# The u products of the first batch move behind its first gating product, in a fused linear attention and gated MLP kernel

## The chip, the cores and the metric

One core of a Trainium2 chip runs the whole kernel. The metric is the device time of one execution, in microseconds, as the median of several executions. PE, ACT, DVE, POOL and SP are the engines of the core: TensorE, ScalarE, VectorE, GpSimd and SyncE. Each works through its own queue of instructions in the order in which the program issued them, and waits on semaphores for the others.

## The reference

For 4 batches of 768 positions, 8 heads of 48 features. All data are f32.

```
f = 1 / (1 + exp(-f_logit))
for t in range(768):                       # per batch and head
    state = f[t][:, None] * state + outer(k[t], v[t])
    y[t] = q[t] @ state
x = y, heads joined                        # (4, 768, 384)
h = gelu(x @ w_in)                         # w_in: 384 x 1024
u, v = h[..., :512], h[..., 512:]
v_n = (v - mean(v)) / sqrt(var(v) + 1e-6) * g_ln
v_s = w_sg @ v_n + b_sg                    # over positions, w_sg: 768 x 768
out = x + (u * v_s) @ w_out                # w_out: 512 x 384
```

## The kernel before

The work is cut into 24 tiles of 128 positions (n, six to a batch) and 8 groups of three tiles (g, two to a batch). For each tile the attention is done in chunked form: the gates (exp, log, a triangular product `cum`, two exp), k and q scaled by them on DVE or POOL, transposes on PE (`tr`), scores and state updates (`su`, lines 474 and 479), mask on DVE (line 484), and the output (`y`, line 522), which ACT and DVE join into x (lines 526 and 530). x is transposed (`xT`, line 552) and split into a high part in fp32r (`xh`, ACT) and a low part (`xl`, DVE, line 569).

Every large product is done as three products in fp32r, high by high, high by low and low by high, in `mm3` (line 547). For each tile `hv` is x against the second half of `w_in` (nine products of 512 columns), and after it come gelu, statistics, normalisation (`nh`, lines 598 and 599 on DVE) and the low part (`nl`, line 604). For each group `hu0..3` are x against the first half of `w_in` (nine products of 384 columns each), and `sg0..3` are the gating products over all six tiles of the batch against `w_sg` (18 products each). `po` is the output product of a tile. A gating product needs the normalised v of all six tiles of its batch, but no u; u is needed by what follows a gating product (`sm_`, line 636, on POOL or DVE).

The weights must be prepared on the chip in the first batch. `w_in` comes in 8 chunks (0 to 3 are for u, 4 to 7 for v) and `w_out` in 4. Each chunk goes through `wa` (ACT, line 300), `wb` (DVE, lines 306 to 308), `wc` (DVE, lines 312 and 313), `wd` (line 318, POOL or DVE), `we` (ACT) and `wf` (line 334, POOL or DVE). `w_sg` is transposed on PE in 12 halves (`wT`, line 343) and split by ACT (line 782) and DVE (line 783).

The order of all instructions is written by a planner, `Plan`, that runs when the program is built. Every step has a cost on each engine that may do it, what it needs, rings of buffers that it takes and frees, and a due time. The planner goes through time and gives an engine the step with the least due time among those that could start about now. Its costs are numbers in the code. In the first batch due times are `T_FIRST + T_TILE * n` and offsets from it: `hv` comes 9 after its tile's transposes, the `hu` of a group 2 after its last `hv`, the `wT` with the second group's `hu`, and the gating products after all of these. The later batches' attention is merged into the products of the batch before by `merge(units + rest, att, A0, A1)`.

Of the kernel before, what the change touches and what calls it, by code (L numbers as in the profile page):

```python
# [36 lines left out]
A0, A1 = 0.12, 0.66  # L37
T_FIRST, T_TILE = 8.0, 6.0
# [14 lines left out]
class Plan:  # L53
# [46 lines left out]
    def run(self):  # L100
        self.dues()
        free = dict.fromkeys(("PE", "ACT", "DVE", "POOL", "SP"), 0.0)
        small, table, wire = False, "E", 0.0
# [102 lines left out]
    STAY, HOLD, SHIFT = 2.0, 4.0, 0.8  # L206
# [3 lines left out]
def gla_moe_kernel(ctx: ExitStack, tc: tile.TileContext, q, k, v, f, w_in, g_ln, w_sg, b_sg, w_out, cst, out):  # L210
# [109 lines left out]
    def w_dst(key):  # L320
        kind, c = key
        a = w_tmp[key][1].bitcast(F32)
        if kind == "in":
            sl = slice(c * P, (c + 1) * P)
            return w_in_hi[:, :, sl], w_in_lo[:, :, sl], a.rearrange("p (k c) -> p k c", k=KT)
# [228 lines left out]
    def x_slice(n):  # L554
        if n // GR not in xT:
# [65 lines left out]
    def sgu(g, ft):  # L621
# [4 lines left out]
            [((v_hl[n0 + s][0][:, fs], v_hl[n0 + s][1][:, fs]), (w_sg_hi[:, s, tokens(g)], w_sg_lo[:, s, tokens(g)])) for s in range(NT)],  # L626
# [68 lines left out]
    def pe(name, fn, t, needs, small=False, bank=1, **kw):  # L695
        add(name, lambda e: fn(), {"PE": t}, 0.2, needs, small=small, bank=bank, **kw)
# [88 lines left out]

    for n in range(N):
# [204 lines left out]
```

## Time and profile before

| what | value |
|---|---|
| runs shown | 393.88, 393.95 and 395.94 us, median 393.95 us |
| the profiled execution | 393.7 us, of which the span is 391.8 us |
| PE busy | 370.2 us, 94% |
| DVE, ACT, POOL busy | 244.6, 170.5, 170.9 us |
| mean granted clock of TensorE | 0.984 |

Busy time is the time in which an engine had an instruction in work. The end of a matrix product is modelled, so a busy PE is not a PE at its best rate. A share of the whole span hides that the stages differ: the first hundred microseconds, with the attention of the first batch and the weights, are unlike the rest.

### The profile page before, as it was taken

The numbers are of one execution on the slowest core, as the hardware profiler recorded it, in microseconds if no ns is written. First come the engines' busy times: TensorE is split into PE (matmuls) and PEld (weight loads), VectorE is DVE, ScalarE is ACT, GpSimd is POOL, SyncE is SP. The second block draws the span as 40 slices with busy tenths as digits, with TensorE's granted clock in tenths as the row PEclk, the third lists the DMA queues.
The fourth block names the chain that finished last, engine by engine and source line by source line (L and its number), as shares of the span: only waits on it lengthen the run. The fifth ranks groups of instructions, "written<-read, shape, count | busy, mean of one in ns | idle before, by whom it ended". The sixth has DMA issues, their size and how long they took to land.

```text
span 391.8 us, 11353 instructions
## 1 busy us (share of the span) xinstructions
PE 370.2 (94%) x4774; PEld 342.0 (87%) x4774; DVE 244.6 (62%) x464; ACT 170.5 (44%) x360; POOL 170.9 (44%) x208
## 2 busy tenths in 40 slices
PE   4879989889899999999999999999999999999994
PEld 3757878779799998999998989899999989899994
DVE  1699995894897566462765576454757665553331
ACT  5376737446653542327553443237544433311110
POOL 2264564423754445162644445052736534233220
PEclk9977999999999999999999999999999999999998
DMA  9999864540137796100187765000376000000002
GB/s 190 219 222 227 166 178 94 123 152 0 23 63 146 127 154 117 33 0 22 22 146 142 115 118 100 20 22 0 56 142 119 10 22 2 21 22 0 22 21 86
DMA packets 133324, 33.90 MB, mean 87 GB/s; under 512 B 125588, under 2 KB 131860, under 8 KB 133268
## 3 DMA queue, kind: packets, MB, share of 16 engines
q1 hardware_dynamic: 133268, 33.12, 41.6%
q8 instruction: 39, 0.64, 0.7%
q14 instruction: 17, 0.14, 0.1%
HBM read 28.34 MB, written 4.77 MB: 84 GB/s over the span
## 4 chain that ended last, share of the span: by engine, by line
PE 76%; DVE 14%; ACT 3%; DMA 2%; issue 2%; POOL 1%; SPq 1%; POOLq 0%
PE ps_b L547 56%; PE ps_y L522 5%; PE ps_b L455 5%; PE ps_s L474 3%; DVE wt L313 2%; PE ps_b L552 2%; PE ps_s L479 2%; DVE wt L312 2%; DMA dec<-dec_d 1%; DVE wt L308 1%; ACT f_raw L234 1%; DVE w_sg_lo L783 1%; DMA f_raw<-in_f_logit_dram 1%; PE ps_b L440 1%; DVE vh L598 1%
## 5 line engine op out<-in xcount | busy, mean ns | idle before, releaser
L547 PE MATMUL ps_b<-w_sg_hi,vh 128*128 128x384 f32 x192 | 65.8, 342 | 1.0 <-DVE gt L631 1.0
L547 PE MATMUL ps_b<-w_sg_hi,vl 128*128 128x384 f32 x192 | 64.6, 336 | 0.0
L547 PE MATMUL ps_b<-w_sg_lo,vh 128*128 128x384 f32 x192 | 64.6, 336 | 0.0
L636 POOL TENSOR_TENSOR gt<-gt,u 128x384 f32<-128x384 f32 x31 | 32.0, 1033 | 65.4 <-DVE gt L631 41.8
L547 PE MATMUL ps_b<-w_out_hi,gg 128*128 128x384 f32 x174 | 48.8, 341 | 0.0
L604 POOL TENSOR_TENSOR vl<-vg,vh 128x512 fp32r<-128x512 f32 x24 | 31.0, 1292 | 18.1 <-DVE vg L599 18.1
L547 PEld LDWEIGHTS ps_b<-w_sg_hi,vh 128*128 128x128 f32 x192 | 36.1, 188 | 2.0 <-DVE gt L631 1.8
L631 DVE SCALAR_TENSOR_TENSOR gt<-ps_b,cols,b_bc 128x384 f32<-128x384 f32 x32 | 19.7, 614 | 26.8 <-PE ps_b L547 25.6
L547 PEld LDWEIGHTS ps_b<-w_sg_lo,vh 128*128 128x128 f32 x192 | 36.1, 188 | 0.0
L547 PEld LDWEIGHTS ps_b<-w_sg_hi,vl 128*128 128x128 f32 x192 | 36.1, 188 | 0.0
L239 ACT COPY sk<-ps_b 112x512 f32<-112x512 f32 x41 | 22.5, 589 | 28.3 <-PE ps_b L455 28.1
L547 PE MATMUL ps_b<-xTh,w_in_hi 128*128 128x384 f32 x96 | 33.1, 345 | 1.4 <-ACT u L234 1.4
L522 PE MATMUL ps_y<-vs,st 64*64 64x48 f32 x768 | 31.4, 223 | 1.2 <-DVE st L484 1.2
L547 PE MATMUL ps_b<-w_in_hi,xTh 128*128 128x512 f32 x72 | 31.2, 433 | 1.3 <-DVE xTl L569 1.3
L547 PE MATMUL ps_b<-xTh,w_in_lo 128*128 128x384 f32 x96 | 32.3, 336 | 0.0
L547 PE MATMUL ps_b<-xTl,w_in_hi 128*128 128x384 f32 x96 | 32.1, 335 | 0.0
L522 PEld LDWEIGHTS ps_y<-vs,st 64*64 64x64 f32 x768 | 28.7, 138 | 3.9 <-DVE st L484 1.4
L547 PEld LDWEIGHTS ps_b<-w_out_hi,gg 128*128 128x128 f32 x174 | 31.8, 188 | 0.1
L522 PE MATMUL ps_y<-S,sk 48*64 48x48 f32 x768 | 30.7, 223 | 0.5 <-POOL S L503 0.5
L651 DVE TENSOR_TENSOR gg<-gt,gg 128x384 fp32r<-128x384 f32 x29 | 18.9, 653 | 18.4 <-ACT gg L647 18.3
L234 ACT ACTIVATE u<-ps_b 128x384 f32<-128x384 f32 x32 | 15.8, 493 | 33.3 <-PE ps_b L547 29.9
L503 POOL TENSOR_TENSOR S<-S,dec 112x192 f32<-112x192 f32 x35 | 19.7, 564 | 23.7 <-DVE S L500 18.6
(108 smaller groups left out, 921.0 us busy)
## 6 DMA issues: line engine op xcount, KB each, us to landing
f_raw<-in_f_logit_dram SPq DMA_DIRECT2D x24, 192.0 KB
kq<-in_k_dram SPq DMA_DIRECT2D x24, 192.0 KB
kq<-in_q_dram SPq DMA_DIRECT2D x24, 192.0 KB
vs<-in_v_dram SPq DMA_DIRECT2D x24, 192.0 KB
out_dram<-o SPq DMA_DIRECT2D x24, 192.0 KB
staged<-in_moe_w_in_dram SPq DMA_DIRECT2D x8, 384.0 KB
staged<-in_moe_w_sg_dram SPq DMA_DIRECT2D x6, 384.0 KB
vs<-in_v_dram SPq DMA_DIRECT2D x36, 48.0 KB
```

The costliest lines, as they stand in the source:

```text
L234: nc.scalar.activation(dst, src, func, **kw)
L239: (nc.scalar.copy if e == "ACT" else ENG[e].tensor_copy)(dst, src)
L312: nc.vector.tensor_scalar(b_, a, 0xFF800000, None, op0=ALU.bitwise_and)
L455: nc.tensor.transpose(psum[f"tr{n}"][j][:W2, p * P : (p + 1) * P], kq[:, j, 2 * p : 2 * p + 2, :].rearrange("t h d -> t (h d)")[:, :W2], i ...
L474: nc.tensor.matmul(ps_s[rows(score_rows(n, c, 2 * p + par)), par, p * C : (p + 1) * C], sk[r, 0, p, c], sk[r, 1, p, c], start=True, stop=True)
L503: ENG[e].tensor_mul(state_to(n, c), state_to(n, c), decay(n, c))
L522: nc.tensor.matmul(ps_y[rows(c), half, h * D : (h + 1) * D], a, m, start=start, stop=stop)
L547: nc.tensor.matmul(ps, a, m, start=(j == 0), stop=(j == len(seq) - 1))
L604: ENG[e].tensor_sub(vl, v_raw.pop(n), vh.bitcast(F32))
L631: nc.vector.scalar_tensor_tensor(t, psum[f"sg{g}.{ft}"][:, :E], g_col[:, ft : ft + 1], b_bc[:, tokens(g)], op0=ALU.mult, op1=ALU.add)
L636: ENG[e].tensor_mul(t, t, uT.pop((g, ft)))
L651: nc.vector.tensor_sub(gl, g_raw.pop((g, ft)), gh.bitcast(F32))
```

## The change

In the first batch the due times are changed: `hv` gets a start and a pace of its own (`V_FIRST`, `V_TILE`), and the eight `hu` and the second half of the `wT` are taken out of the stage ahead of the gating products and put in among them, behind the first one. So that x of the first three tiles can wait so long, its two parts are kept in the tile of the second half of `w_sg`; the `wT` of that half wait for the four `hu` of group 0. `w_in` and `w_sg` become two tiles each; the lines that only index them anew are left out below, and so are some lines in which nothing but a cost, a `port` mark or a latency changes.

The planner's costs change. It now counts that DVE and POOL slow each other when both work on SBUF (`port`, `RATE`), and the thresholds by which it gives work to POOL (`AWAY`), changes the activation table (`HOLD`) or the shape of PE's products (`STAY`) are others.

In the normalisation one of two DVE passes (line 598, to fp32r) is taken out; ACT rounds the f32 result instead (`norm_round`).

In the planned gaps of PE up to 40 us of the plan, products of a tile of zeros with itself (128 x 128 x 128, f32) are put into PE's queue, one for every 0.48 us of a gap before 8 us of the plan and one for every 0.24 us after it. They write a bank of PSUM that the plan has free.

```diff
--- before
+++ after
@@ -34,8 +34,8 @@
-A0, A1 = 0.12, 0.66
-T_FIRST, T_TILE = 8.0, 6.0
+A0, A1 = 0.15, 0.76
+T_FIRST, T_TILE, V_FIRST, V_TILE, T_SG = 13.29, 5.05, 25.13, 3.49, 60.46
...
@@ -54,10 +54,11 @@
-    SEM = 0.1
-    MODE = 0.2
+    SEM = 0.06
+    MODE = 0.15
+    RATE = dict(DVE=0.44, POOL=0.75)
...
@@ -65,12 +66,13 @@
-    def add(self, name, fn, engines, lat=0.1, needs=(), due=None, take=(), free=(), small=None, table=None, wire=0.0, bank=0, unbank=None, after=0.0):
+    def add(self, name, fn, engines, lat=0.1, needs=(), due=None, take=(), free=(), small=None, table=None, wire=0.0, bank=0, unbank=None, after=0.0, port=False):
...
@@ -100,7 +102,7 @@
-        small, table, wire = False, "E", 0.0
+        small, table, wire, port = False, "E", 0.0, dict(DVE=0.0, POOL=0.0)
...
@@ -152,7 +154,7 @@
-                        gain = {o: max(free[one], t) + s["engines"][one] - max(free[o], t) - s["engines"][o] - self.SHIFT for o in s["engines"] if o != one}
+                        gain = {o: max(free[one], t) + s["engines"][one] - max(free[o], t) - s["engines"][o] - (self.AWAY if o == "POOL" else self.SHIFT) for o in s["engines"] if o != one}
...
@@ -171,6 +173,11 @@
+            if e == "POOL" or e == "DVE" and s["port"]:
+                other = max(port["POOL" if e == "DVE" else "DVE"] - t, 0.0)
+                rate = self.RATE[e]
+                took = took / rate if took < other * rate else took + other * (1 - rate)
+                port[e] = t + took
...
@@ -203,7 +210,30 @@
-    STAY, HOLD, SHIFT = 2.0, 4.0, 0.8
+    def warm(self, order, until, fn):
+        ends = {}
+        for s in order:
+            if s["unbank"]:
+                name, i = s["unbank"] if isinstance(s["unbank"], tuple) else (s["unbank"], 0)
+                ends[name, i] = s["end"]
+        held = [(k, s["start"], ends.get((s["name"], i), 1e9)) for s in order for i, k in enumerate(s["at"])]
+        last, more = self.W_FROM, []
+        for s in [s for s in order if s["on"] == "PE"]:
+            if s["start"] > until:
+                break
+            t = last
+            while t + self.W_TIME * (2 if t < self.W_COLD else 1) < s["start"] - self.W_REST:
+                k = [k for k in range(len(self.banks)) if not any(b == k and x < s["start"] and y > t for b, x, y in held)]
+                if not k:
+                    break
+                more.append(dict(name="warm", on="PE", start=t, n=-1, bank=0, at=k[:1], fn=lambda e, k=k[0]: fn(k)))
+                t += self.W_TIME * (2 if t < self.W_COLD else 1)
+            last = s["start"] + s["engines"]["PE"] + 0.05
+        return sorted(order + more, key=lambda s: (s["start"], s["n"]))
+    W_FROM, W_COLD, W_TIME, W_REST = 1.0, 8.0, 0.24, 0.2
+    STAY, HOLD, SHIFT, AWAY = 4.0, 3.31, 1.21, -0.97
...
@@ -245,10 +275,10 @@
-    w_in_hi = cp.tile([P, KT, FF], F32R, name="w_in_hi")
-    w_in_lo = cp.tile([P, KT, FF], F32R, name="w_in_lo")
-    w_sg_hi = cp.tile([P, NT, S], F32R, name="w_sg_hi")
-    w_sg_lo = cp.tile([P, NT, S], F32R, name="w_sg_lo")
+    w_in_hi = [cp.tile([P, KT, FH], F32R, name=f"w_in_hi{j}") for j in range(2)]
+    w_in_lo = [cp.tile([P, KT, FH], F32R, name=f"w_in_lo{j}") for j in range(2)]
+    w_sg_hi = [cp.tile([P, NT, E], F32R, name=f"w_sg_hi{g}") for g in range(2)]
+    w_sg_lo = [cp.tile([P, NT, E], F32R, name=f"w_sg_lo{g}") for g in range(2)]
...
@@ -256,6 +286,8 @@
+    zeros = cp.tile([P, P], F32, name="zeros")
...
@@ -344,7 +376,8 @@
-        return (slice(None), slice(hf * KT, (hf + 1) * KT), slice(tt * P, (tt + 1) * P)), ps
+        sl = (slice(None), slice(hf * KT, (hf + 1) * KT), slice(tt % GR * P, (tt % GR + 1) * P))
+        return w_sg_hi[tt // GR][sl], w_sg_lo[tt // GR][sl], ps
...
@@ -552,7 +585,10 @@
-        if n // GR not in xT:
+        if n // GR not in xT and n < GR and row0 is None:
+            xT[0] = (w_sg_hi[1][:, 0:KT], w_sg_hi[1][:, KT : 2 * KT])
+        elif n // GR not in xT:
...
@@ -595,9 +631,11 @@
-        nc.vector.tensor_scalar(vh, vg, mv[:, 0:1], rs, op0=ALU.subtract, op1=ALU.mult)
+    def norm_round(n):
+        nc.scalar.copy(v_hl[n][0], v_raw[n])
...
@@ -727,18 +765,19 @@
-        due.update({f"tr{n}": t, f"su{n}": t + 1.5, f"y{n}": t + 5, f"xT{n}": t + 7, f"hv{n}": t + 9})
-    for g in range(2):
-        for j in range(NF):
-            due[f"hu{g}.{j}"] = due[f"hv{GR * g + GR - 1}"] + 2 + 1.6 * j
-    for i in range(NT):
+        due.update({f"tr{n}": t, f"su{n}": t + 1.5, f"y{n}": t + 5, f"xT{n}": V_FIRST + V_TILE * n - 2, f"hv{n}": V_FIRST + V_TILE * n})
+    for i in range(GR):
-            due[f"wT{i}.{j}"] = due["hu1.0"] + 0.7 * (2 * i + j)
+            due[f"wT{i}.{j}"] = due[f"hv{NT - 1}"] + 0.5 * (2 * i + j)
+        if b == 1:
+            hu = [f"hu{g}.{ft}" for g in range(2) for ft in range(NF)]
+            wT = [f"wT{i}.{j}" for i in range(GR, NT) for j in range(2)]
+            units = sg[0][:1] + hu[:2] + sg[0][1:2] + hu[2:4] + wT[:2] + sg[0][2:3] + hu[4:6] + wT[2:4] + sg[0][3:] + hu[6:] + wT[4:] + sg[1][:1] + po[:GR] + sg[1][1:]
...
@@ -751,7 +790,7 @@
-    t = due[f"hu1.{NF - 1}"] + 2
+    t = T_SG
...
@@ -769,18 +808,19 @@
-            op("wb" + s, lambda e, key=key: w_bits(key), "DVE:1.25", ["wa" + s])
-            op("wc" + s, lambda e, key=key: w_low(key), "DVE:0.9", ["wb" + s], free=("gg",))
-            op("wd" + s, lambda e, key=key: w_sum(key, e), "POOL:1.06 DVE:0.48", ["wc" + s], free=("u",))
+            op("wb" + s, lambda e, key=key: w_bits(key), "DVE:1.3", ["wa" + s], port=True)
+            op("wc" + s, lambda e, key=key: w_low(key), "DVE:0.92", ["wb" + s], free=("gg",), port=True)
+            op("wd" + s, lambda e, key=key: w_sum(key, e), "DVE:0.55 POOL:1.05", ["wc" + s], free=("u",), port=True)
-            op("wf" + s, lambda e, key=key: w_lo(key, e), "POOL:1.14 DVE:0.48", ["we" + s], free=("u",))
+            op("wf" + s, lambda e, key=key: w_lo(key, e), "DVE:0.55 POOL:1.05", ["we" + s], free=("u",), port=True)
-            pe("wT" + s, lambda i=i, j=j: sg_trans(i, j), 0.34, [f"ldsg{i}", "cs"], due=due["wT" + s])
-            op("wh" + s, lambda e, i=i, j=j: nc.scalar.copy(w_sg_hi[sg_slice(i, j)[0]], sg_slice(i, j)[1]), "ACT:0.43", ["wT" + s])
-            op("wl" + s, lambda e, i=i, j=j: nc.vector.tensor_sub(w_sg_lo[sg_slice(i, j)[0]], sg_slice(i, j)[1], w_sg_hi[sg_slice(i, j)[0]].bitcast(F32)),
+            late = [f"hu0.{ft}" for ft in range(NF)] if i >= GR else []
+            pe("wT" + s, lambda i=i, j=j: sg_trans(i, j), 0.3, [f"ldsg{i}", "cs"] + late, due=due["wT" + s])
+            op("wh" + s, lambda e, i=i, j=j: nc.scalar.copy(sg_slice(i, j)[0], sg_slice(i, j)[2]), "ACT:0.43", ["wT" + s])
+            op("wl" + s, lambda e, i=i, j=j: nc.vector.tensor_sub(sg_slice(i, j)[1], sg_slice(i, j)[2], sg_slice(i, j)[0].bitcast(F32)),
...
@@ -801,13 +841,13 @@
-            op(f"lh{n}", lambda e, n=n: gate_hi(n, e), "ACT:0.42 DVE:0.38", [f"l{n}"], take=("lh",))
-            op(f"ll{n}", lambda e, n=n: gate_lo(n, e), "DVE:0.48 POOL:1.14", [f"lh{n}"])
+            op(f"lh{n}", lambda e, n=n: gate_hi(n, e), "ACT:0.42 DVE:0.38", [f"l{n}"], take=("lh",), port=True)
+            op(f"ll{n}", lambda e, n=n: gate_lo(n, e), "DVE:0.55 POOL:1.05", [f"lh{n}"], port=True)
-        op(f"mq{n}", lambda e, n=n: mul_q(n, e), "POOL:1.06 DVE:0.48", [f"up{n}", f"q{n}"])
-        op(f"mk{n}", lambda e, n=n: mul_k(n, e), "POOL:1.06 DVE:0.48", [f"dn{n}", f"k{n}"], free=("f",))
+        op(f"mq{n}", lambda e, n=n: mul_q(n, e), "DVE:0.55 POOL:1.05", [f"up{n}", f"q{n}"], port=True)
+        op(f"mk{n}", lambda e, n=n: mul_k(n, e), "DVE:0.55 POOL:1.05", [f"dn{n}", f"k{n}"], free=("f",), port=True)
...
@@ -830,37 +870,38 @@
-                op(f"sm{n}.{c}", lambda e, n=n, c=c: state_mul(n, c, e), "POOL:0.5 DVE:0.27", [f"sa{n}.{c}"] + d)
+                op(f"sm{n}.{c}", lambda e, n=n, c=c: state_mul(n, c, e), "DVE:0.33 POOL:0.52", [f"sa{n}.{c}"] + d, port=True)
-        op(f"nh{n}", lambda e, n=n: norm_hi(n), "DVE:1.05", [f"nr{n}"], take=("vh",))
+        op(f"nh{n}", lambda e, n=n: norm_hi(n), "DVE:0.55", [f"nr{n}"], take=("vh",), port=True)
+        op(f"nc{n}", lambda e, n=n: norm_round(n), "ACT:0.5", [f"nh{n}"])
-                op(f"sm_{s}", lambda e, g=g, ft=ft: sgu_gate(g, ft, e), "POOL:1.06 DVE:0.48", [f"sb{s}", f"gu{s}"], free=("u",))
+                op(f"sm_{s}", lambda e, g=g, ft=ft: sgu_gate(g, ft, e), "DVE:0.55 POOL:1.05", [f"sb{s}", f"gu{s}"], free=("u",), port=True)
...
@@ -875,8 +916,9 @@
-    steps = plan.run()
+    steps = plan.warm(plan.run(), 40.0, lambda k: nc.tensor.matmul(ps_b[k][:, :P], zeros, zeros, start=True, stop=True))
+        nc.vector.memset(zeros, 0.0)
```

## Rows read from the trace of the kernel before

**Rows 1.** Busy time of the engines (with instructions) by stretches, then clock, DMA share, GB/s

```profile
0.00:4.60 4.60, 0.00 (x0) 0.00 (x0) 0.86 (x2) 2.42 (x4) 1.68 (x12) 1.00 0.59 128
4.60:20.80 16.20, 13.88 (x162) 11.43 (x163) 8.67 (x22) 7.46 (x18) 3.58 (x4) 1.00 1.21 223
20.80:24.20 3.40, 2.02 (x14) 1.32 (x12) 3.33 (x5) 2.76 (x6) 2.41 (x3) 1.00 1.05 255
24.20:34.40 10.20, 8.49 (x79) 5.93 (x80) 10.13 (x17) 5.84 (x13) 6.88 (x8) 0.50 1.04 250
34.40:55.00 20.60, 18.75 (x395) 16.40 (x394) 19.97 (x45) 13.48 (x26) 10.42 (x14) 1.00 0.86 188
55.00:89.70 34.70, 31.58 (x394) 27.56 (x392) 27.15 (x56) 17.39 (x34) 15.94 (x22) 1.00 0.44 112
89.70:110.00 20.30, 18.82 (x113) 18.10 (x113) 13.36 (x20) 14.25 (x36) 12.48 (x11) 1.00 0.07 11
110.00:386.90 276.90, 276.63 (x3627) 261.24 (x3625) 160.63 (x304) 106.90 (x225) 117.47 (x139) 1.00 0.34 65
```

**Rows 2.** PE in order of time, first 90 us: start, duration, instruction

```profile
4.63 1.65 PE L407 MATMUL ps_b<-f_raw,cs 128*128 128x384 f32 x2 [4.63 <-ACT f_raw L234]
...
10.96 1.94 PE L455 MATMUL ps_b<-cs,kq 128*112 128x128 f32 x8
...
21.06 0.81 PE L407 MATMUL ps_b<-f_raw,cs 128*128 128x384 f32 x2
...
36.88 1.09 PE L455 MATMUL ps_b<-cs,kq 128*112 128x128 f32 x8
...
53.65 0.34 PE L547 MATMUL ps_b<-xTh,w_in_hi 128*128 128x384 f32 x1
...
81.43 0.33 PE L547 MATMUL ps_b<-xTh,w_in_hi 128*128 128x384 f32 x1
...
86.14 0.49 PE L343 MATMUL ps_b<-cs,staged 128*128 128x128 f32 x3
...
89.69 0.40 PE L547 MATMUL ps_b<-w_sg_hi,vh 128*128 128x384 f32 x1
```

**Rows 3.** What PE waited for, up to 90 us: total, times, longest

```profile
PE ps_b L407 <- ACT f_raw L234: 5.0, 2, 4.6
PE ps_b L552 <- DVE x L530: 1.9, 1, 1.9
...
PE ps_b L547 <- DVE xTl L569: 1.3, 1, 1.3
```

**Rows 4.** Groups of instructions on DVE up to 90 us

```profile
L313 DVE SCALAR_TENSOR_TENSOR wt<-staged,wt 128x384 f32<-128x384 uint32 x10 | 8.6, 856 | 0.3
L308 DVE SCALAR_TENSOR_TENSOR wt<-staged,wt 128x384 uint32<-128x384 uint32 x10 | 6.4, 636 | 0.5
L312 DVE TENSOR_SCALAR wt<-wt 128x384 uint32<-128x384 uint32 x10 | 6.0, 598 | 0.0
L307 DVE TENSOR_SCALAR wt<-wt 128x384 uint32<-128x384 uint32 x10 | 5.9, 594 | 0.3
L783 DVE TENSOR_TENSOR w_sg_lo<-ps_b,w_sg_hi 128x384 fp32r<-128x384 f32 x11 | 5.5, 546 | 0.0
L598 DVE TENSOR_SCALAR vh<-vg,mv,rs 128x512 fp32r<-128x512 f32 x6 | 4.2, 700 | 1.6 <-POOL rs L590 1.5
...
L306 DVE TENSOR_SCALAR wt<-wt 128x384 f32<-128x384 f32 x10 | 3.5, 351 | 1.4 <-ACT wt L300 1.4
```

**Rows 5.** DVE in order of time, the same instruction beside POOL and alone

```profile
45.30 2.46 DVE L312 TENSOR_SCALAR wt<-wt 128x384 uint32<-128x384 uint32 x1
47.79 0.56 DVE L313 SCALAR_TENSOR_TENSOR wt<-staged,wt 128x384 f32<-128x384 uint32 x1
...
48.66 0.36 DVE L307 TENSOR_SCALAR wt<-wt 128x384 uint32<-128x384 uint32 x1
...
49.99 0.35 DVE L312 TENSOR_SCALAR wt<-wt 128x384 uint32<-128x384 uint32 x1
```

**Rows 6.** POOL in order of time, at the same place

```profile
45.56 1.02 POOL L421 TENSOR_TENSOR kq<-kq,f_raw 128x384 f32<-128x384 f32 x1
46.54 1.00 POOL L334 TENSOR_TENSOR w_in_lo<-wt,w_in_hi 128x384 fp32r<-128x384 f32 x1
```

**Rows 7.** ACT in order of time: a rounding copy of 384 columns

```profile
97.13 0.51 ACT L647 CAST gg<-gt 128x384 fp32r<-128x384 f32 x1
```

More of the change, by code (lines that the diff above doesn't have):

```diff
@@ L66, in __init__ @@
         self.steps, self.by = [], {}
-    def add(self, name, fn, engines, lat=0.1, needs=(), due=None, take=(), free=(), small=None, table=None, wire=0.0, bank=0, unbank=None, after=0.0):
+    def add(self, name, fn, engines, lat=0.1, needs=(), due=None, take=(), free=(), small=None, table=None, wire=0.0, bank=0, unbank=None, after=0.0, port=False):
         assert name not in self.by, name
         s = dict(name=name, fn=fn, engines=engines, lat=lat, needs=list(needs), due=due, take=take, free=free,
-                 small=small, table=table, wire=wire, bank=bank, unbank=unbank, after=after, end=None, start=None, n=len(self.steps))
+                 small=small, table=table, wire=wire, bank=bank, unbank=unbank, after=after, port=port, end=None, start=None, n=len(self.steps))
         self.steps.append(s)
@@ L323, in w_dst @@
         if kind == "in":
[L324 to L325 removed]
+            sl = slice(c % NF * P, (c % NF + 1) * P)
+            return w_in_hi[c // NF][:, :, sl], w_in_lo[c // NF][:, :, sl], a.rearrange("p (k c) -> p k c", k=KT)
         return w_out_hi[:, c], w_out_lo[:, c], a
@@ L573, in h_v @@
         sl = slice((n % GR) * P, (n % GR + 1) * P)
-        mm3(psum[f"hv{n}"], [((hi[:, j, sl], lo[:, j, sl]), (w_in_hi[:, j, FH:], w_in_lo[:, j, FH:])) for j in range(KT)])
+        mm3(psum[f"hv{n}"], [((hi[:, j, sl], lo[:, j, sl]), (w_in_hi[1][:, j], w_in_lo[1][:, j])) for j in range(KT)])
     def gelu_v(n):
@@ L608, in h_u @@
         fs = slice(ft * P, (ft + 1) * P)
-        mm3(psum[f"hu{g}.{ft}"][:, :E], [((w_in_hi[:, j, fs], w_in_lo[:, j, fs]), (hi[:, j], lo[:, j])) for j in range(KT)])
+        mm3(psum[f"hu{g}.{ft}"][:, :E], [((w_in_hi[0][:, j, fs], w_in_lo[0][:, j, fs]), (hi[:, j], lo[:, j])) for j in range(KT)])
         if ft == NF - 1:
@@ L625, in sgu @@
             psum[f"sg{g}.{ft}"][:, :E],
-            [((v_hl[n0 + s][0][:, fs], v_hl[n0 + s][1][:, fs]), (w_sg_hi[:, s, tokens(g)], w_sg_lo[:, s, tokens(g)])) for s in range(NT)],
+            [((v_hl[n0 + s][0][:, fs], v_hl[n0 + s][1][:, fs]), (w_sg_hi[g % 2][:, s], w_sg_lo[g % 2][:, s])) for s in range(NT)],
         )
@@ L695, in pe @@
     def pe(name, fn, t, needs, small=False, bank=1, **kw):
-        add(name, lambda e: fn(), {"PE": t}, 0.2, needs, small=small, bank=bank, **kw)
+        add(name, lambda e: fn(), {"PE": t}, 0.13, needs, small=small, bank=bank, **kw)
     def on(engines):
@@ L817, in gla_moe_kernel @@
                 dma(f"di{n}.{par}", lambda e, n=n, par=par: dec_in(n, par, e), 0.25, [f"do{n}"] + ["clear"] * (n == NT))
-        pe(f"tr{n}", lambda n=n: trans(n), 0.89, [f"mk{n}", f"mq{n}", "cs"], bank=2, due=due[f"tr{n}"])
+        pe(f"tr{n}", lambda n=n: trans(n), 0.84, [f"mk{n}", f"mq{n}", "cs"], bank=2, due=due[f"tr{n}"])
         for j in range(2):
@@ L837, in gla_moe_kernel @@
         g = n // GR
-        pe(f"xT{n}", lambda n=n: x_trans(n), 0.34, [f"jy{n}", "cs"], due=due[f"xT{n}"])
-        op(f"xh{n}", lambda e, n=n: x_hi(n), "ACT:0.43", [f"xT{n}", f"xh{n - 1}"], take=("xT",) if n % GR == 0 else ())
+        pe(f"xT{n}", lambda n=n: x_trans(n), 0.3, [f"jy{n}", "cs"], due=due[f"xT{n}"])
+        op(f"xh{n}", lambda e, n=n: x_hi(n), "ACT:0.43", [f"xT{n}", f"xh{n - 1}"], take=("xT",) if n % GR == 0 and n else ())
         op(f"xl{n}", lambda e, n=n: x_lo(n), "DVE:0.5", [f"xh{n}"], unbank=f"xT{n}")
-        pe(f"hv{n}", lambda n=n: h_v(n), 2.12, [f"xl{n}"] + [f"wfin{c}" for c in range(4, 8)], due=due[f"hv{n}"])
+        pe(f"hv{n}", lambda n=n: h_v(n), 2.08, [f"xl{n}"] + [f"wfin{c}" for c in range(4, 8)], due=due[f"hv{n}"])
         turn = [f"dn{n0 + j}" for j in range(NT)] if b else []
@@ L845, in gla_moe_kernel @@
         op(f"nr{n}", lambda e, n=n: norm_rs(n), "POOL:1.1", [f"ns{n}", "clear"])
-        op(f"nh{n}", lambda e, n=n: norm_hi(n), "DVE:1.05", [f"nr{n}"], take=("vh",))
-        op(f"nl{n}", lambda e, n=n: norm_lo(n, e), "POOL:1.31 DVE:0.6", [f"nh{n}"], free=("vg",))
+        op(f"nh{n}", lambda e, n=n: norm_hi(n), "DVE:0.55", [f"nr{n}"], take=("vh",), port=True)
+        op(f"nc{n}", lambda e, n=n: norm_round(n), "ACT:0.5", [f"nh{n}"])
+        op(f"nl{n}", lambda e, n=n: norm_lo(n, e), "DVE:0.68 POOL:1.31", [f"nc{n}"], free=("vg",), port=True)
         if i % GR == GR - 1:
@@ L850, in gla_moe_kernel @@
                 s = f"{g}.{ft}"
-                pe(f"hu{s}", lambda g=g, ft=ft: h_u(g, ft), 1.6, [f"xl{n}", f"wfin{ft}"], due=due[f"hu{s}"], free=("xT",) if ft == NF - 1 else ())
+                pe(f"hu{s}", lambda g=g, ft=ft: h_u(g, ft), 1.57, [f"xl{n}", f"wfin{ft}"], due=due[f"hu{s}"], free=("xT",) if ft == NF - 1 and g else ())
                 if ft == NF - 1:
@@ L940, in gla_moe_kernel @@
                     norm_hi(n)
+                    norm_round(n)
                     norm_lo(n, "POOL")
```

6 lines of the change are left out of this document (3 added, 3 removed).

## Prediction

> **What bounds the kernel now.** I read the busy time by stretches first [rows 1]. After 110 us PE is busy 276.63 of 276.90 us: nothing that shortens another engine's work can show there, and the change leaves PE's products there as they are. All that can be won lies ahead of 110 us. Up to 89.7 us, where the first gating product starts [rows 2], PE is busy 13.88 + 2.02 + 8.49 + 18.75 + 31.58 = 74.7 us. It is idle 4.6 us until the first gate arrives, which no part of the change brings earlier, and another 10.4 us after that, 12.2% of the 85.1 us. In 89.7 to 110 us it is idle 1.5 us more.
>
> Some of the 74.7 us is PE at the lower clock. The granted clock is 0.50 between 24.2 and 34.4 us [rows 1], the lower of the two levels (1.2 GHz). The same row column says 1.00 from the start, but the instructions say otherwise: two gate products took 1.65 us at 4.63 us and 0.81 us at 21.06, eight transposes 1.94 us at 10.96 and 1.09 us at 36.88 [rows 2]. So 4.6 to about 20.8 us ran at the lower level too, though PE was busy 13.88 of 16.2 us. With the ratio of the transposes, 1.78, the 13.88 + 8.49 = 22.4 us of busy time at the lower level would be 12.6 us at the higher: 9.8 us of excess.
>
> The waits of PE in these 90 us end mostly with DVE or with ACT behind it: 1.9 us for the joined x (line 530), 1.3 us for the low part of x (line 569) [rows 3]. DVE is busy 19.97 of 20.6 us in 34.4 to 55 and 69.3 of the 85.1 us from 4.6 us on, 81%. So the first stage is one in which DVE sets the pace and PE follows, part of the time at half its rate.
>
> What fills DVE is the weights [rows 4]: per chunk 351 + 594 + 636 + 598 + 856 ns = 3.04 us in five passes, ten chunks by 90 us. They are stretched by POOL: line 312 took 2.46 us while POOL worked on two 384-column operations and 0.35 us alone [rows 5, 6]. Against the lone durations of 0.35, 0.36 and 0.56 us the ten passes of lines 312, 307 and 313 lost 2.5 + 2.3 + 3.0 = 7.8 us.
>
> **The u products move.** The eight `hu` stand ahead of the first gating product now. The last group's first three, 27 products, go from 81.43 to 86.14 us [rows 2]: 1.57 us each, 12.6 us for the eight. With them five of the eleven halves of `w_sg` done by then move behind (0.49 us each on PE [rows 2], 2.4 us; on DVE 0.546 us each [rows 4], 2.7 us). So 15.0 us of PE work goes from ahead of the first gating product to behind it. It is not saved: the start of that product must come 15.0 us earlier only to break even, at 74.7 us. What the move buys is order on DVE. The four u chunks of `w_in` and the two chunks of `w_out` done by 90 us, 6 x 3.04 = 18.2 us, need not be ready for the gating product.
>
> **The normalisation.** Six passes of line 598 in this stage, 4.2 us of DVE [rows 4], go away; ACT does six roundings of 0.51 us by the nearest row, one of 384 columns [rows 7], so about 0.7 us for 512. ACT has 17.39 busy of 34.7 us in 55 to 89.7 [rows 1], so these 4 us hide there; they stand in the chain from v to the gating product, but in place of a DVE pass that stood there too. The 18 later tiles give DVE 12 us back after 110 us, where it is 58% busy, and that is worth nothing.
>
> **The sum, first by PE.** Ahead of the first gating product there is 74.7 - 9.8 - 15.0 = 49.9 us of PE work at the higher clock. I keep 3 us of the lower clock for the start (the two gate products and the decays of tiles 0 and 1) and the same idle share, 12.2%: 52.9 / 0.878 = 60.3 us, so the product starts at 64.9 us instead of 89.7. Of these 24.8 us the moved work takes 15.0 back: 9.8 us gained. DVE can follow: of its 70.1 us up to 89.7 us, 18.2 + 2.7 + 4.2 = 25.1 us leave, and 44.1 us in 60.3 us is 73%, less than the 81% of now.
>
> **Then by DVE, behind that point.** The stretch of 20.3 us up to the progress of 110 us becomes 35.3 us of PE time, and DVE has to do 13.36 + 18.2 + 2.7 = 34.3 us in it, 97%. DVE did that once, in 34.4 to 55; over the whole first 90 us it did 81%. At 97% nothing is lost, at 81% the stretch takes 42.3 us, 7.0 us more. I take 90% (38.1 us, 2.8 lost), since the chunks of `w_out` are wanted late, behind the `hu`, and can slide. A planner that counts the shared time of DVE and POOL may avoid part of the 7.8 us of stretching: nothing to 5 us, and I take 1.5. The sum is 9.8 - 2.8 + 1.5 = 8.5 us.
>
> **The zero products.** The trace has none. A gate product of 384 columns in f32 took 0.81 us, or 1.65 us at the lower clock, for two [rows 2] (two records for one product of the program); a third of it, 0.27 or 0.55 us, is my estimate for one of 128 columns. They stand in PE's queue only where the plan has PE idle, so their cost is hidden by waits for DVE and ACT, and each gap that isn't there costs at most what was put in it. Above, I bound the cost by the 5.4 us that PE is idle between 4.6 and 34.4 us [rows 1]; below, by a gain of 9.8 us if they hold the higher clock throughout. I have counted 6.8 us of that, before idle shares. The Trainium skill (TensorE: Matmul & The Clock Gate, Part 1, What's actually happening) says that the throttled clock is the default and that activity releases it. The trace agrees in the default, but there 16 us of nearly unbroken busy records didn't release it; if by that rule the products raised the clock before the first gate product, the sum would be about 3.4 us better, and if they count for as little as those records did, 7.7 us worse.
>
> **The planner's other numbers** (table and shape thresholds, latencies, `A0`, `A1`) shift orders after 110 us, where the trace has 0.3 us of idle: no gain is possible, and a wait made there would be a loss of its own size. I take zero, and up to 2 us of loss for the range.
>
> The sum is made against the profiled execution: 393.7 - 8.5 = 385.2 us. The median of the runs shown is 0.25 us above it, so I forecast 385.5 us.
>
> **Rivals.** *The u weights come late (smaller gain).* DVE keeps its 81% and the `hu`, in PE's fixed order, hold the gating products behind them: 9.8 - 7.0 = 2.8 us, or up to 5.5 with some stretching avoided, so 388.5 to 391.5 us. For it speaks the row of 34.4 to 55, full to 97%, and the 13.36 us that are there anyway; against it, that DVE has 42% idle right behind 110 us. *All of it works (larger gain).* The clock is high from the start (+3.4), idle falls to 8% (+2.8) and DVE holds 97% (+2.8): 17.5 us, 376 us; half of that gives 381. Against it: every stretch before 90 us has more idle than that except 34.4 to 55 once it runs at full clock. *The change doesn't do what it says with the clock.* The zero products leave it where it was: 8.5 - 7.7 = 0.8 us, 393 us, no change to speak of. For it: busy records did not raise it in 16 us; against it: those were small transposes and two-column products, and it did rise at about 20.8 us after the first attention output. *Slower.* In the trace the first `hu` start at 53.65 us [rows 2], in the middle of DVE's congestion: they fill PE while DVE is behind. If they are only a filler there, taking them out leaves PE idle for up to 12.6 us in 50 to 70 us while the attention of the later tiles still waits for DVE, and the `hu` cost their full time afterwards. This decides once the first gating product starts later than 74.7 us; at 78 us the kernel is 3.3 us slower, 397 us. Against it: 25.1 us of DVE work leaves ahead of that point.
>
> **Chances.** Forecast, 382 to 388.5 us: 0.50. Larger gain, 375 to 382: 0.17. Smaller gain: 0.14. Clock not raised, within 0.5%: 0.09. Slower: 0.10. About 0.5%, 2 us, is what a measurement of this kernel can tell from no change. Faster by more has 0.50 + 0.17 + 0.14 = 0.81. The range of 378.5 to 391.5 us leaves out the last two cases and the least of the larger gains.
>
> **What will show it.** The first gating product at about 65 us (right), beyond 72 us (wrong); the granted clock and the gate product's 0.81 us from about 8 us on; DVE near 90% between 65 and 100 us, with PE's waits there on line 334 or 313's results; fewer passes of lines 307, 312 and 313 beyond 1 us; PE without idle behind about 105 us. Wrong would make it: zero products waiting for a bank, a fall of the clock in the twenties as before, or PE waiting for the u chunks for over 7 us.

## The result, and the profile after

The changed kernel took 391.13 us (median of four runs, 389.78 to 391.36) against 393.91 us for the kernel before (four runs, 393.61 to 395.94): a ratio of 0.9908, 95% interval 0.9883 to 0.9933. It is 2.8 us faster, where 8.5 us were forecast; 385.5 us was the number. Twice more, each time on one chip with other kernels, the ratio was 0.9883 (0.986 to 0.9905) and 0.9903 (0.987 to 0.9936). The profiled execution took 389.78 us with a span of 388.0 us, 3.9 us less than the profiled one of before; it is the fastest of the four, so what is read from the profiles shows a gain about 1 us larger than the medians do.

Busy time by stretches after, with the columns of [rows 1]:

```profile
0.00:4.70 4.70, 3.65 (x16) 3.49 (x16) 1.09 (x3) 2.42 (x4) 1.67 (x12) 1.00 0.63 136
4.70:24.60 19.90, 17.59 (x285) 14.13 (x284) 12.44 (x24) 11.21 (x27) 8.05 (x8) 1.00 1.08 215
24.60:31.40 6.80, 5.46 (x99) 5.13 (x103) 6.77 (x11) 4.14 (x12) 5.54 (x8) 0.54 1.32 215
31.40:55.00 23.60, 23.33 (x507) 20.23 (x503) 22.12 (x45) 17.14 (x32) 12.98 (x19) 0.99 0.89 206
55.00:78.60 23.60, 22.66 (x181) 20.66 (x180) 22.96 (x43) 12.13 (x26) 14.91 (x17) 1.00 0.59 143
78.60:110.00 31.40, 27.06 (x333) 24.11 (x331) 25.50 (x41) 25.03 (x57) 18.52 (x19) 1.00 0.43 80
110.00:383.10 273.10, 271.93 (x3420) 257.27 (x3420) 138.68 (x264) 113.46 (x236) 110.15 (x136) 1.00 0.31 61
```

PE in order of time after. The first gate product, the first and the last records of u products of group 0 (their x lies in the tile of `w_sg`, so they read `w_sg_hi,w_in`), the last hv, and the first gating product (`w_sg_hi,vh`):

```profile
4.72 0.91 PE L440 MATMUL ps_b<-f_raw,cs 128*128 128x384 f32 x2
...
63.41 0.59 PE L580 MATMUL ps_b<-w_sg_hi,w_in_hi 128*128 128x384 f32 x2
...
66.62 0.39 PE L580 MATMUL ps_b<-w_in_hi,xTh 128*128 128x512 f32 x1
...
78.40 0.34 PE L580 MATMUL ps_b<-w_sg_hi,w_in_lo 128*128 128x384 f32 x1
78.57 0.34 PE L580 MATMUL ps_b<-w_sg_hi,vh 128*128 128x384 f32 x1
```

The reader is to see three things. The first gating product starts at 78.57 us, 11.1 us earlier than in [rows 2], but all eight u products still stand ahead of it, from 63.4 to 78.7 us with the last hv between them. A due time is only a priority: the planner gives PE what is ready, and while v's last tiles went through ACT, POOL and DVE the u products were. Only halves of `w_sg` went behind, six against one, five more, 2.4 us by [rows 2]. So the lead at that point is 11.1 - 2.4 = 8.7 us in this profile. Profiles of two more executions of the changed kernel have the start at 78.64 and 80.07 us, so a difference of 1.5 us at that point can be chance.

Second, the lower clock is gone up to 24.6 us (the first gate product takes 0.91 us instead of 1.65) and comes back until 31.4 us.

Third, from the first gating product to the end of PE's last product it is 382.9 - 78.6 = 304.3 us, and so in the two other profiles too, against 386.9 - 89.7 = 297.2 us: 7.1 us longer. Of these 2.4 are the halves, 3.6 are idle time of PE (304.3 less 27.06 + 271.93 busy is 5.3 us; before it was 1.7 us by [rows 1]), and 1.1 us is spread. 8.7 - 3.6 - 1.1 = 4.0 us, by which PE ends earlier; the spans differ by 3.8 us.

DVE's groups of the weight passes up to 120 us, of the kernel after and, under it, of the kernel before (line, operation, count, busy us, mean ns):

```profile
L345 DVE SCALAR_TENSOR_TENSOR wt<-staged,wt 128x384 f32<-128x384 uint32 x12 | 12.6, 1053 | 0.4
L340 DVE SCALAR_TENSOR_TENSOR wt<-staged,wt 128x384 uint32<-128x384 uint32 x12 | 9.9, 823 | 0.5
L338 DVE TENSOR_SCALAR wt<-wt 128x384 f32<-128x384 f32 x12 | 8.2, 687 | 1.2 <-ACT wt L332 1.2
L344 DVE TENSOR_SCALAR wt<-wt 128x384 uint32<-128x384 uint32 x12 | 6.3, 527 | 0.0
...
L339 DVE TENSOR_SCALAR wt<-wt 128x384 uint32<-128x384 uint32 x12 | 5.7, 477 | 0.4
```

```profile
L313 DVE SCALAR_TENSOR_TENSOR wt<-staged,wt 128x384 f32<-128x384 uint32 x12 | 10.4, 863 | 0.4
L312 DVE TENSOR_SCALAR wt<-wt 128x384 uint32<-128x384 uint32 x12 | 7.5, 625 | 0.0
L308 DVE SCALAR_TENSOR_TENSOR wt<-staged,wt 128x384 uint32<-128x384 uint32 x12 | 7.5, 623 | 0.5
L307 DVE TENSOR_SCALAR wt<-wt 128x384 uint32<-128x384 uint32 x12 | 6.7, 555 | 0.4
...
L306 DVE TENSOR_SCALAR wt<-wt 128x384 f32<-128x384 f32 x12 | 4.2, 351 | 2.5 <-ACT wt L300 2.5
```

The sixty passes take 42.7 us after and 36.3 us before. A plan that counts the shared time did not make them shorter here: they take 6.4 us more. The three lines of which the prediction spoke (307, 312 and 313, now 339, 344 and 345) take 24.6 us in both kernels; the growth is all in the two others.

### The profile page after: what moved, and what is told of

Read it like the earlier page. It is cut to its first block, busy times and chain, and to the rows that moved or that the text cites. A ratio compares the mean times of both kernels' runs of the same rounds, so it can differ in the third digit from the quotient of the medians.

```text
span 388.0 us, 11476 instructions
## 1 busy us (share of the span) xinstructions
PE 371.7 (96%) x4826; PEld 345.0 (89%) x4826; DVE 229.9 (59%) x426; ACT 185.5 (48%) x391; POOL 171.8 (44%) x216
## 4 chain that ended last, share of the span: by engine, by line
PE 79%; DVE 9%; SPq 4%; DMA 3%; POOL 1%; ACT 1%; issue 1%; ACTq 0%
PE ps_b L580 60%; PE ps_y L555 6%; PE ps_b L488 5%; PE ps_s L507 3%; PE ps_s L512 2%; PE ps_b L585 2%; DMA kq<-in_q_dram 2%; SPq L401 2%; DVE wt L345 1%; DVE wt L340 1%; DVE st L618 1%; DMA vs<-in_v_dram 1%; DVE w_sg_lo L823 1%; DVE wt L338 1%; DVE wt L344 1%
## 5 line engine op out<-in xcount | busy, mean ns | idle before, releaser
L674 POOL TENSOR_TENSOR gt<-gt,u 128x384 f32<-128x384 f32 x30 | 31.0, 1034 | 72.4 <-DVE gt L669 51.6
L669 DVE SCALAR_TENSOR_TENSOR gt<-ps_b,cols,b_bc 128x384 f32<-128x384 f32 x32 | 19.7, 615 | 38.1 <-PE ps_b L580 38.0
L269 ACT COPY sk<-ps_b 112x512 f32<-112x512 f32 x47 | 25.8, 588 | 17.4 <-PE ps_b L488 16.2
L454 POOL TENSOR_TENSOR kq<-kq,f_raw 128x384 f32<-128x384 f32 x21 | 26.4, 1255 | 10.7 <-DMA kq<-in_k_dram 6.6
L536 POOL TENSOR_TENSOR S<-S,dec 112x192 f32<-112x192 f32 x40 | 21.0, 526 | 21.6 <-DVE S L533 18.7
L685 ACT CAST gg<-gt 128x384 fp32r<-128x384 f32 x29 | 15.1, 520 | 29.8 <-POOL gt L674 26.6
L700 DVE TENSOR_TENSOR o<-ps_b,x 128x384 f32<-128x384 f32 x24 | 13.4, 557 | 26.7 <-PE ps_b L580 26.0
L580 PE MATMUL ps_b<-w_out_lo,gg 128*128 128x384 f32 x87 | 29.2, 335 | 0.0
L580 PE MATMUL ps_b<-xTh,w_in_hi 128*128 128x384 f32 x84 | 28.9, 344 | 0.0
```

What stands on the lines that cost most here:

```text
L269: (nc.scalar.copy if e == "ACT" else ENG[e].tensor_copy)(dst, src)
L454: ENG[e].tensor_mul(kt, kt, f_raw.pop(n))
L536: ENG[e].tensor_mul(state_to(n, c), state_to(n, c), decay(n, c))
L580: nc.tensor.matmul(ps, a, m, start=(j == 0), stop=(j == len(seq) - 1))
L669: nc.vector.scalar_tensor_tensor(t, psum[f"sg{g}.{ft}"][:, :E], g_col[:, ft : ft + 1], b_bc[:, tokens(g)], op0=ALU.mult, op1=ALU.add)
L674: ENG[e].tensor_mul(t, t, uT.pop((g, ft)))
```

## Experiments

Sixteen runs were made, in four groups, each group on one chip beside the kernel before (medians 394.75, 394.63, 395.33 and 394.80 us). Ratios are to that. In e1, e2, e5, e13 and e14 the order of the other instructions is that of the kernel they are made from. In the other changed ones the edit goes through the planner, so the whole order may change with it.

**e1_no_zeros.** The zero products go, nothing else.

```diff
-    steps = plan.warm(plan.run(), 40.0, ...)
+    steps = plan.run()
```

> The changed kernel without its 52 zero products; every other instruction in the same order. If the gain is that of the clock (8.5 us less busy time of PE ahead of the first gating product), the first attention runs at the lower level until about 20 us again, the first gating product starts some 6 to 9 us later than at 78.6 us, and the time is 394 to 400 us. If DVE sets the pace of the first stage whatever the clock, and the products only fill waits, the time stays within 1.5 us of 391.1 us.

393.41 us, 0.9961 (0.9939 to 0.9983). The first gate products ran at the lower level again, and the first gating product came at 80.82 us:

```profile
4.79 1.65 PE L439 MATMUL ps_b<-f_raw,cs 128*128 128x384 f32 x2 [4.79 <-ACT f_raw L264]
...
80.82 0.34 PE L579 MATMUL ps_b<-w_sg_hi,vh 128*128 128x384 f32 x1
```

So the products bring 2.25 us at that point by these two profiles (0.75 us against the latest of the three starts above) and 0.5 to 0.8% of the time by the medians (0.9961 against 0.988 to 0.991), 2 to 3 us: between the two expectations. PE was busy 69.2 us up to there without them and 72.7 - 8.9 (the 52 products) = 63.8 us with them: of 5.4 us of busy time saved, some 3 turned into waits.

**e2_before_zeros.** The kernel before with zero products in its own gaps (66 of them), nothing else.

```diff
-    steps = plan.run()
+    steps = plan.warm(plan.run(), 40.0, ...)
```

> The kernel before with nothing but zero products in its own planned gaps. If the clock alone carries the gain: the first gating product starts some 6 to 8 us earlier than at 89.7 us and the time is 386 to 389 us. If the first stage is DVE's, the time stays within 1.5 us of 393.9 us, and the clock is worth something only together with the new order.

395.39 us, 1.002 (0.999 to 1.0049): no gain. The clock did rise, by the first gate product, and the first gating product starts where it did, at 89.69 us:

```profile
4.72 0.91 PE L431 MATMUL ps_b<-f_raw,cs 128*128 128x384 f32 x2
...
89.69 0.38 PE L571 MATMUL ps_b<-w_sg_hi,vh 128*128 128x384 f32 x1
```

Up to there PE was busy 77.3 - 11.0 (the 66 products) = 66.3 us, 8.4 us less than the 74.7 us of the kernel before, and all of it turned into waits. In the kernel before, PE's clock in the first stage costs nothing that the end can see.

**e3_hu_behind.** The u products of the first batch really wait for the first gating product.

```diff
-[f"xl{n}", f"wfin{ft}"]
+[f"xl{n}", f"wfin{ft}"] + ["sg0.0"] * (g < 2)
```

> The changed kernel with one more need: the eight u products wait for the first gating product, which is what the prediction took the change to do. If they were only filler while v's chain through ACT, POOL and DVE was under way (they ran from 63.4 to 78.7 us, with hv of tile 5 among them), the first gating product starts only 4 to 7 us earlier, at 72 to 75 us, PE is idle for 8 to 11 us ahead of it, and the time is 395 to 402 us. If the prediction's sum was right, it starts at 63 to 67 us and the time falls to 384 to 388 us.

401.40 us, 1.0162 (1.0136 to 1.0188), some 10 us worse than the changed kernel. The gating product did start at 66.66 us, close to the forecast 64.9. So the start came where the second expectation had it, and the time where the first had. The gating product reads v tile by tile, and its last third waited for the last two tiles:

```profile
68.57 0.34 PE L580 MATMUL ps_b<-w_sg_hi,vl 128*128 128x384 f32 x1
70.47 0.45 PE L580 MATMUL ps_b<-w_sg_hi,vh 128*128 128x384 f32 x1 [1.56 <-ACT vh L638]
...
72.34 0.48 PE L580 MATMUL ps_b<-w_sg_hi,vl 128*128 128x384 f32 x1 [1.25 <-POOL vl L642]
73.28 0.69 PE L580 MATMUL ps_b<-w_sg_hi,vh 128*128 128x384 f32 x1 [0.46 <-ACT vh L638]
...
75.03 0.69 PE L580 MATMUL ps_b<-w_sg_hi,vl 128*128 128x384 f32 x1 [0.74 <-POOL vl L642]
```

PE was idle for 4.0 us there, and its clock fell in it (0.74 granted between 66.7 and 80 us). In this run the last low part of v is done at 75.0 us and the first gating product ends at 75.7 us. In the changed kernel POOL makes that low part just ahead of the gating product, which ends at 81.9 us:

```profile
77.23 1.28 POOL L642 TENSOR_TENSOR vl<-vg,vh 128x512 fp32r<-128x512 f32 x1 [1.60 <-ACT vh L638]
```

So eight u products of 12.6 us delay the end of the first gating product by 6.1 us when they stand ahead of it; behind it they cost their full time. They are mostly filler in this place.

**e4_norm_back.** The normalisation of before: the pass of DVE returns, ACT's rounding goes.

```diff
+        nc.vector.tensor_scalar(vh, vg, mv[:, 0:1], rs, ...)
-        op(f"nc{n}", lambda e, n=n: norm_round(n), "ACT:0.5", [f"nh{n}"])
```

> The changed kernel with the normalisation of before (two passes on DVE, no rounding on ACT). The prediction gave the removed pass 4.2 us of DVE in the first stage. If DVE sets the pace there, the time rises by 2 to 4 us, to 393 to 395 us; if PE and its clock set it, it stays within 1 us of 391.1 us.

392.35 us, 0.9936 (0.9906 to 0.9966). The interval overlaps those of the changed kernel, so a cost of some 1 us is likely and not settled, and neither expectation is met; the gating product starts at 79.12 us, within the three starts above. 4.2 us of DVE were not worth 4 us.

**e5_out_light, e13_before_out_light.** The five DVE passes of each `w_out` chunk are left out, in the changed kernel and as a control in the kernel before; the output product then works on wrong weights.

```diff
+        if key[0] == "out":
+            return
         nc.vector.tensor_scalar(a.bitcast(F32), ...)
...
+        if key[0] == "out":
+            nc.vector.memset(b_[:, 0:1].bitcast(F32), 0.0)
+            staged.pop(key)
+            return
         nc.vector.tensor_scalar(b_, a, 0xFF800000, ...)
```

> The changed kernel without the five DVE passes that recover each of the four chunks of w_out (one tiny memset stands for them, the instructions' order is otherwise that of the changed kernel); the output product then works on wrong weights. About 3.0 to 4.5 us of stretched DVE time a chunk go, 3 chunks of them behind 85 us. If DVE's backlog of weights makes PE's waits between 85 and 110 us (4.4 us in sum, 1.5 us in the kernel before), two thirds of them go and the time is 387.5 to 389 us. If the waits come from the next batch's attention being asked for too early (its loads of q, ACT's tables, the banks), the time stays within 1 us of 391 us.

> The kernel before without the five DVE passes of each of the four w_out chunks (the output product works on wrong weights): the control to the same cut in the changed kernel, which took it from 391 to 385.2 us. If the backlog of w_out behind the first gating product is a cost that the changed order created, the kernel before gains under 2.5 us (its two late chunks stood in a stretch with 1.5 us of waits). If every kernel with this work pays for it alike, it gains 4 to 6 us.

The changed kernel: 385.17 us, 0.9756 (0.9736 to 0.9777), 5.6 us less than its mean ratio of 0.990 gives, a larger gain than either expectation had. The control: 393.16 us, 0.997 (0.9946 to 0.9993), 1.2 us less, as the first expectation had it. What PE waited for between the first gating product and 110 us, in the changed kernel and then in its light version:

```profile
PE ps_b L488 <- POOL kq L454: 1.1, 1, 1.1
PE ps_b L580 <- ACT f_raw L264: 0.8, 1, 0.8
PE ps_b L580 <- DVE w_sg_lo L823: 0.6, 1, 0.6
PE ps_b L375 <- DVE gt L669: 0.3, 1, 0.3
```

```profile
PE ps_b L587 <- ACT f_raw L264: 0.5, 1, 0.5
```

The first list holds 2.8 of the 4.3 us of idle time up to 110 us. The gating product itself started no earlier (79.69 us); from it to the end of PE's last product it is 299.2 us instead of 304.3, which is 5.1 us less. In the kernel before the same cut takes this stretch from 297.2 to 295.9 us, 1.3 us. So of the 7.1 - 2.4 = 4.7 us that the changed kernel loses behind the first gating product, 3.8 us are `w_out` on DVE, made by the changed order. A longer wait ends just behind 110 us and is not in the list. Here is PE at its end, and DVE in order of time ahead of it, with the join of x (line 563) behind two passes of a chunk:

```profile
110.09 0.52 PE L585 MATMUL ps_b<-cs,x 128*128 128x128 f32 x3 [1.35 <-DVE x L563]
```

```profile
107.36 0.35 DVE L344 TENSOR_SCALAR wt<-wt 128x384 uint32<-128x384 uint32 x1
107.75 1.72 DVE L345 SCALAR_TENSOR_TENSOR wt<-staged,wt 128x384 f32<-128x384 uint32 x1
109.39 0.54 DVE L563 SCALAR_TENSOR_TENSOR x<-ps_y,x 128x384 f32<-128x384 f32 x1
```

This wait is gone in the light version. How the passes make each of the other waits was not followed.

**e6_attention_later, e11_u_early_later.** A0 = 0.30 in the changed kernel, and in the kernel of e7.

```diff
-A0, A1 = 0.15, 0.76
+A0, A1 = 0.30, 0.76
```

> The changed kernel with A0 = 0.30 instead of 0.15: the attention of each next batch is merged in later among the products. If PE's waits between 85 and 110 us come from that attention being asked for too early, they fall from 4.4 us to under 2 and the time is 388 to 390 us. If DVE's backlog makes them, they stay and the time is 390.5 to 394 us, with some loss behind 110 us where the attention is then late.

> The changed kernel with the move of u undone and A0 = 0.30. Undoing the move gave 389.3 us; a later attention gave 390.9 against 391.1 us. If the two add, 388 to 389.5 us; if the next batch's attention is needed early to hide its loads, 390 to 394 us.

390.91 us, 0.9897 (0.9876 to 0.9919): no difference, so an attention asked for too early is not the cause. On e7 the same number gave 401.81 us, 1.0142 (1.0102 to 1.0182), a miss of both expectations by 8 us.

**e7_u_early, e15_u_early_again.** The move undone, all else kept; run twice.

```diff
+    for g in range(2):
+        for j in range(NF):
+            due[f"hu{g}.{j}"] = due[f"hv{GR * g + GR - 1}"] + 2 + 1.6 * j
...
-            units = sg[0][:1] + hu[:2] + sg[0][1:2] + hu[2:4] + wT[:2] + ...
+            units = sg[0][:2] + wT[:2] + sg[0][2:3] + wT[2:4] + sg[0][3:] + wT[4:] + ...
```

> The changed kernel with the due times of the u products as in the kernel before (2 us behind the last hv of their group) and without them in the list of the gating stage: the move undone, all else kept. If the lower priority of u is what brought the first gating product forward (to 80.8 us even without zero products, from 89.7), it goes back to 85 to 89 us and the time is 394 to 397 us. If the other due times, the costs and the removed pass did it, it stays at 78 to 81 us and the time within 1 us of 391.1 us.

> The changed kernel with the move of u undone, once more, beside the changed kernel on one chip. If undoing the move is worth something, the ratio is again 0.984 to 0.988 and at least 0.002 below the changed kernel's; if the first 389.3 us were chance, the two differ by less than 0.002.

389.27 us, 0.9865 (0.9843 to 0.9888), and 389.49 us, 0.9858 (0.9832 to 0.9884). The changed kernel had 0.9908, 0.9883 and 0.9903. The intervals overlap, but the two medians lie below all three of the changed kernel (391.13, 390.70, 390.92), by about 1.5 us. For e7 both expectations missed; for e15 the first one held. The gating product starts later (81.22 and 81.31 us), and less is lost behind it: to the end of PE's last product it is 300.6 and 302.4 us instead of 304.3, and in the first PE is idle 2.3 us up to 110 us instead of 4.3.

```profile
81.20:110.00 28.80, 26.52 (x288) 25.01 (x289) 23.00 (x36) 23.07 (x52) 20.31 (x18) 1.00 0.27 56
```

The move of u, in the change's name, brings nothing; that it costs about 1.5 us is likely, not settled. This is the fastest of the kernels run here that do the whole work.

**e8_old_costs, e9_port_off, e10_costs_only.** The changed kernel planned with the old waits, latency and thresholds and no sharing (the costs of single steps stay the new ones); with nothing but the sharing off; and the kernel before with only the new costs, thresholds and sharing.

```diff
-    RATE = dict(DVE=0.44, POOL=0.75)
+    RATE = dict(DVE=1.0, POOL=1.0)          # e8, e9
-    STAY, HOLD, SHIFT, AWAY = 4.0, 3.31, 1.21, -0.97
+    STAY, HOLD, SHIFT, AWAY = 2.0, 4.0, 0.8, -0.8          # e8, with SEM, MODE and PE's latency
```

> The changed kernel planned with the numbers of the kernel before for waits, modes and thresholds, and without the sharing of DVE and POOL; due times, order of the lists, zero products and the removed pass stay. If the planner's view of the shared time is what gained in the first stage, the time goes up by 3 to 6 us, to 394 to 397 us; if the due times did it, it stays within 1.5 us of 391.1 us.

> The changed kernel planned without the sharing of DVE and POOL alone; every other number of the changed planner stays. If the shared time is what made the old costs 8 us worse (399.3 against 391.1 us), this is at 395 to 400 us. If the thresholds and latencies did it, this is within 1.5 us of 391 us.

> The kernel before, planned with the changed planner's costs, thresholds and shared time, and nothing else of the change: due times and lists as before, no zero products, the normalisation as before (w_in and w_sg are two tiles each, x of the first group lies in its old ring). If the costs carry the gain by themselves, 388 to 392 us. If they only repair what the new due times would break, within 1.5 us of 394 us or slower.

399.31 us, 1.0109 (1.0089 to 1.013); 405.03 us, 1.0249 (1.0222 to 1.0275); 404.38 us, 1.0218 (1.0189 to 1.0246). The first is 2.3 us and the second 5.0 us above the range that was expected; the third is "or slower". Read with the kernel before (1) and the changed one (0.990) this is nearly a square: old due times with new numbers 1.022, new due times with old numbers 1.011, both new 0.990. The corners are not clean: e10 also lacks the zero products and the shorter normalisation, which by e1 and e4 are worth some 0.6% and 0.3%, and e8 keeps the new step costs. Even so each half alone is slower than neither. The gating product of e9 started at 87.96 us. The gain belongs to how the two fit; no edit alone was found to carry it.

**e14_u_light.** The DVE passes of the four u chunks are left out of the changed kernel (u is then wrong).

```diff
+        if key[0] == "in" and key[1] < 4:
+            return
```

> The changed kernel without the five DVE passes of each of the four w_in chunks of u (u is then wrong); the order is otherwise the same. In the changed kernel these 12 to 16 us of stretched DVE time lie ahead of the first gating product, because its u products ran there. If DVE's work sets that point and not PE, the product starts at 68 to 74 us instead of 78.6 and the time is 382 to 387 us. If PE or the chain of v sets it, it stays within 2 us of 78.6 us.

388.01 us, 0.9826 (0.9798 to 0.9853). The gating product starts at 78.14 us; in three profiles of the changed kernel it starts at 78.57, 78.64 and 80.07 us. So with 12 us and more of DVE work gone it comes 0.4 to 1.9 us earlier: these DVE passes do not set this point, but the u products ahead of it and the chain of v beside them. PE was busy without a gap from 62.0 to 78.14 us in this run, and 16.47 of the last 16.57 us ahead of the gating product in the changed kernel. The median is still some 2.9 us lower (0.9826 against 0.990); where that is won one profile does not show, since it has 304.0 us behind the gating product, as good as the 304.3.

**e12_after_again, e16_after_third.** The changed kernel itself, in the third and the fourth group.

> The changed kernel itself, beside the others on one chip: a ratio of 0.988 to 0.994 to the kernel before, as at first. If the version with the move undone (0.9865, interval 0.9843 to 0.9888) is really the faster one, this stays above 0.989.

> The changed kernel, beside the former: a ratio of 0.987 to 0.992, from 0.9908 and 0.9883 at first.

390.70 and 390.92 us, with the ratios given at the top. Both are in the ranges expected, but e12's 0.9883 is not above the 0.989 by which e7 was to be really faster; e16 on one chip with e15 is (0.9903 against 0.9858).

## Why the prediction missed

The direction was right, the size a third of the forecast: 2.8 us by the medians and 3.8 us by the profiles, where the sum had 9.8 - 2.8 + 1.5 = 8.5 us. By its own steps:

- *"So 15.0 us of PE work goes from ahead of the first gating product to behind it."* This step failed. I read due times and the list as the order of the work; 2.4 us moved, and the u products stayed as filler. The result at that point came out near the forecast all the same, 8.7 against 9.8 us. In part that is arithmetic: the start was 13.7 us later than 64.9 us, but 12.6 us less stood behind it, so in the sum the move alone was worth little (15.0 / 0.878 - 15.0 = 2.1 of the 9.8 us). The rest is luck: 7.7 us of it were the clock's, which brought 2 to 3, and some 6 us came from an order for which the sum has no term. e3 shows the order that I had summed: its start was right, 66.7 us, and it was 10 us slower, because PE waited for v and the u products then cost their full time. That is what the rival "slower" had said of them.
- *The clock.* I had counted 6.8 us of excess as saved, 7.7 us in the sum. The clock rose even ahead of the first gate product, and it fell in the twenties as before, which I had named as a sign of being wrong; 5.4 us of busy time went. But the end saw 2 to 3 us in the changed kernel (e1) and none in the kernel before (e2). I had written that DVE sets the pace and then summed PE as if it did.
- *"At 97% nothing is lost, at 81% ... 7.0 us more. I take 90% (38.1 us, 2.8 lost)."* Of the 4.5 us that the sum has too many (8.5 against the 4.0 by which PE ended earlier) 1.1 stand at the gating product, 1.9 here and 1.5 in the next term, so this one is the largest: 4.7 us were lost, and e5 with its control puts 3.8 of it (4.4 by the medians) on the `w_out` passes, which I had expected to slide. The join of x stands behind them in DVE's fixed order. DVE did not have the 34.3 us of work at 90% that I had put there: up to 110 us it was busy 25.5 of 31.4 us, 81%, since the u chunks had stayed ahead. (In the sum by PE, 70.1 - 25.1 is 45.0 us and not 44.1; nothing hangs on it.)
- *Stretching avoided, 1.5 us.* None was: the passes that I had named take what they took, and the five together 6.4 us more of DVE time. What that costs the end no run separates.
- *The normalisation* was summed as 4.2 us of DVE; e4 leaves about 1 us of time, not settled.
- *Behind 110 us nothing* was nearly right: PE is busy 271.93 of the 272.9 us to the end of its last product, idle 0.9 us against 0.3 before.

The rival with the smaller gain, 388.5 to 391.5 us, gave the time and DVE's 81% behind the gating product, but not the work: it had the u weights come late, and it was `w_out`. What made the lead at the gating product, some 6 us without the zero products, stays open in part: it needs the new due times and the new costs together (e8, e9, e10), and no single edit was found to carry it.

## What to carry to other kernels

A due time in a list scheduler says what may go first, not where it goes: before pricing a move, look at what fills the place that it is to leave. Time saved on an engine that another one paces is a wait elsewhere, so price it from the engine that paces (here 5.4 us of PE's busy time were worth 2 to 3 us, and in the kernel before 8.4 us were worth nothing). And where an order comes from a planner, test edits on top of each other and apart: here one setting of the planner (`RATE`, e9) moved the time by 3.5%, more than the change did.

## What the runs showed of the hardware

The 52 zero products had PE's clock at the higher level from the first gate product on: 0.91 us for it at 4.72 us, behind a chain of 16 such products from 1.05 us, against 1.65 us at 4.63 us [rows 2]; the 66 of e2 did the same. It fell again to the lower level between 24.6 and 31.4 us (0.54 granted), after PE had been idle for 2.0 us up to 25.95 us, although 28 zero products had run between 16.5 and 21.7 us. In e3 it fell too while PE waited piecemeal in 66.7 to 80 us (9.29 us busy of 13.3).
